# Chunked attention, then a routed expert layer, on one core: another order at the beginning and in the expert loop, w2 loaded later, the first routing spread

## The chip, the cores and the metric

The kernel runs on one core of a Trainium2 chip. The metric is the device time of one execution in microseconds (us), the median of three runs; lower is better. A profile is one further execution, recorded by the hardware profiler.

## The reference

q, k and v have 8 batches, 8 heads, 576 positions and 64 columns, all float32. Attention is local: each chunk of 64 positions attends to itself alone. The heads joined give x (8 x 576 tokens of 512 columns). Each token then goes through one of eight experts:

```python
scores = scale * q_c @ k_c^T ; scores -= max ; attn = exp(scores) / (sum + 1e-9)
x = (attn @ v_c), heads joined: [8, 576, 512]
logits = x @ w_gate                        # [8, 576, 8]
local_gate = sigmoid(x @ w_local)          # [8, 576]
for b, s in order:
    fresh_e = argmax(logits[b, s])
    e = fresh_e if s == 0 or local_gate[b, s] < 0.5 else prev_e
    p = softmax(logits[b, s])
    out[b, s] = p[e] * (relu(x[b, s] @ w1[e]) @ w2[e])   # 512 -> 1024 -> 512
```

Which expert a token gets may hang on the tokens before it, so the routing is a scan.

## The kernel before

**Attention.** The 4608 tokens are 18 tiles of 256 (`NS`). A tile is loaded (`load_qk`, `load_v`, issued by SyncE, SP), q and k are copied so that two heads lie side by side (`a_pair`), transposed by TensorE (PE) and copied out of PSUM (`a_tq`), multiplied to scores, which VectorE (DVE) reduces and shifts and ScalarE (ACT) exponentiates (`a_sa`); the probabilities are transposed (`a_tp`), multiplied with v and normalised (`a_va`), the result is transposed (`a_tx`) and multiplied with the router's columns (`a_ra`), which also stores the tile's rows, logits included, in the DRAM table `x_d`. Tiles 4 and 13 collect the last 64 positions of four batches: their loads and stores come in four small pieces.

**Orders by hand.** Within `manual_schedule` the engines named there execute in the order of the program text. The text is given by strings in `PAR`: `play` takes names of queues and counts, and runs the next atoms of each. `PAR["start"]` is the beginning (tiles 0 to 2), `PAR["steady"]` one step of the loop over i = 1 to 15 (scores of tile i + 1, transposes of tile i + 2, values of tile i - 1, router of tile i - 2), `PAR["drain"]` what follows. PE, DVE and ACT are in that order in all parts, GpSimd (POOL) from the loop on; SP's order is the scheduler's until the expert loop. Letters such as `"AVPA"` in `PAR` say which engine copies (A ACT, V DVE, P POOL).

**First routing.** The first half of the tokens (`TA` = 18 groups of 128) is routed while attention still runs (`route`, with the atoms s1a to s11, then ranks, then one-hot rows). A step of the loop has four places for such work, h0 to h3; `PAR["hooks"]` lists for each piece the step and place as 4 i + h. Then three early tiles of expert 0 are gathered from `x_d` (`early_gather`), whose expert work is done within the drain.

**Weights.** Expert 0's w1 (`raw1`) is loaded after steps 6, 8, 10 and 12 and its w2 (`raw2`, four loads of 512 KB) after steps 13 and 14. Products of float32 precision are made of three passes: a weight is held as a high part (`w1h`, `w2h`, a copy by ACT) and a low part (`w1l`, `w2l`, a difference by DVE or POOL), and so are the activations. `w2_split` in the drain (queue w) makes the parts of expert 0's w2 and loads the next expert's w2 into `raw2`.

**Expert loop.** The tokens are sorted by expert into tiles of 128 rows, in halves of 64; a tile whose halves belong to two experts is mixed. Tile t's step (`step`) does the first product and relu of tile t, the gather of tile t + 2, the high and low parts of the next tile's x (`next_x`), the second product, scaling by the probability and scatter of tile t - 1 (`down`), and h's parts of tile t. Registers read from `regs` say whether the expert changes (row 0), which expert comes (row 1), whether a tile is there at all (row 2, from tile 36, `TMIN`, on) and whether it is mixed (row 3); what hangs on them stands in `tc.If`, on the engines that it uses. `either` chooses between the mixed and the plain products, `rejoin` builds the operands of a mixed tile, `refill` renews the weights' high and low parts where the expert changes and loads the next ones. With these inputs there are 38 tiles, 3 of them mixed.

Of the kernel before, what the change touches and what calls it, by code (L numbers as in the profile page):

```python
# [40 lines left out]
    "start": (  # L41
        "p0*4 t0a*4 t0a t0b*4 t0b t0c*4 t0c t0d*4 t0d p1*4 q3 t1a*4 t1a t1b*4 t1b s0*8 s0*2 t1c*4 t1c "
        "q4 t1d*4 t1d p2*4 s0*4 s1*8 t2a*4 t2a t2b*4 t2b s1*4 o0*4 o0*4 o0 s1*2 t2c*4 o0 t2c t2d*4 t2d q5 p3*4 "
    ),
# [17 lines left out]
    "steady": "lq s*8 s h0 tx*8 s va*4 va tq*8 ra*2 h1 tq*8 va*4 lv va ra*2 h2 tp*8 s pr*4 h3 ",  # L62
    "hooks": [43, 43, 44, 45, 46, 47, 48, 48, 50, 50, 52, 52, 54, 54, 55, 58, 61, 61, 62],
}
# [3 lines left out]
def tile_attention_then_moe(ctx: ExitStack, tc, q, k, v, wg, wl, w1, w2, out):  # L68
# [430 lines left out]
    def run(fns):  # L499
        for fn in fns:  # L500
            fn()

    for t in vbuf:
        nc.gpsimd.memset(t[:, :, :, D:DV], 1.0)
# [7 lines left out]
    nc.sync.dma_start(wg9[:, :, 8:9], wl.rearrange("(c p) e -> p c e", p=P))  # L512
    with tc.manual_schedule(engines=MAN):
        def load(store, fn, i):
            def go():
                store[i] = fn(i)
            return lambda: [go]

        tqs = {}

        def tq(i, g):
            if i not in tqs:
                tqs[i] = a_tq(i, ENG(PAR[f"t{i}"]))
# [3 lines left out]
        st |= dict(  # L527
            s0=lambda: a_sa(0, True), q3=load(qk, load_qk, 3),
            s1=lambda: a_sa(1, True), o0=lambda: a_tp(0, True), q4=load(qk, load_qk, 4), q5=load(qk, load_qk, 5))
# [5 lines left out]
    def iota(shape, pattern, base=0, cm=0, dt=F32, name=None, dst=None):  # L535
        t = cpool.tile(shape, dt, name=name) if dst is None else dst
        nc.gpsimd.iota(t, pattern, base=base, channel_multiplier=cm, allow_small_or_imprecise_dtypes=True)
        return t

    pcol = iota([P, 1], [[0, 1]], cm=1, name="pcol")  # L540
    pcol1 = iota([P, 1], [[0, 1]], base=1, cm=1, name="pcol1")
    iota_r = iota([P, P], [[1, P]], dst=pa2.tile([P, P], BF16, name="iota_r", tag="xT", bufs=1))
    iota_m = iota([P, P], [[0, 2], [1, HT]], dt=BF16, name="iota_m")
    iota_h = iota([P, 2, NTILE], [[1, 2], [2, NTILE]], dt=BF16, name="iota_h")
    iota_hp = cpool.tile([P, NTILE], BF16, name="iota_hp")
    for r in range(2):
        nc.gpsimd.iota(iota_hp[HT * r:HT * r + HT], [[2, NTILE]], base=r, channel_multiplier=0,
                       allow_small_or_imprecise_dtypes=True)
    iota_t = cpool.tile([P, NT], BF16, name="iota_t")
    for ph in range(2):  # L550
        iota(None, [[9, 4], [4, 2], [2, 2]], base=36 * ph, dst=iota_t[:, TA * ph:TA * ph + TA - 2])
        for cp in range(2):
            iota(None, [[9, 2]], base=36 * ph + 18 * cp + 8 - cp,
                 dst=iota_t[64 * cp:64 * cp + 64, TA * ph + TA - 2:TA * ph + TA])
    iota_e = iota([P, E], [[1, E]], name="iota_e")
    idxm8 = iota([P, E], [[1, E]], base=-E, name="idxm8")
    padidx = iota([P, NTILE], [[P, NTILE]], base=2 * N, cm=1, name="padidx")
    upper = pa1.tile([P, P], BF16, name="upper")
    nc.vector.tensor_scalar(upper, iota_r, pcol, None, ALU.is_gt)
    ones = pa1.tile([P, P], BF16, name="ones")  # L560
    nc.gpsimd.memset(ones, 1.0)
    zrow = pa1.tile([P, E * NT], F32, name="zrow")
    nc.gpsimd.memset(zrow, 0.0)
    notfirst = pa1.tile([P, NT], F32, name="notfirst")
    nc.gpsimd.memset(notfirst, 1.0)
    for b in range(B):
        t = TA * (b // 4) + 4 * (b % 4)
        nc.gpsimd.memset(notfirst[0:1, t:t + 1], 0.0)


# [144 lines left out]
    def either(mix, plain, both):  # L715
        if mix is None:
            plain()
            return
        with tc.If(mix != 0) as cmp:
            both()  # L720
        with cmp.Else():
            plain()

# [75 lines left out]

    hot0 = cpool.tile([P, E], F32, name="hot0")  # L800
    nc.gpsimd.memset(hot0, 0.0)
    nc.gpsimd.memset(hot0[:, 0:1], 1.0)

    sg, sg_rank, sg_onehots = route(0, TA, lambda t: nc.gpsimd if t % 2 else nc.vector)
# [7 lines left out]

    hq = sg + [lambda: run(sg_rank()), after_a, lambda: run(sg_onehots())] + sl[:2] + [early_gather] + sl[2:]
    hooks = {}
# [4 lines left out]
    for i in range(1, NS - 2):  # L819
# [8 lines left out]
        if i in (6, 8, 10, 12):  # L828
            load_w1(0, i // 2 - 3)
        if i in (13, 14):  # L830
            for c in range(2 * i - 26, 2 * i - 24):
                load_w2(0, c)
        if 8 <= i < 16:
# [8 lines left out]


    n = NS - 1
    sa = a_sa(n, True)
# [71 lines left out]
    def rejoin(mix, parts, names, last):  # L917
# [7 lines left out]
        pair = pool.tile([P, len(parts), 4, P], F32R, name="pair" + names[0], **tag)  # L925
        with tc.If(mix != 0):  # L926
            for g, part in enumerate(parts):
                for n, a in enumerate(part):
                    V.tensor_copy(pair[:, g, :, HT * n:HT * n + HT], a[:, :, 0:HT])
            for full, (hi, lo) in zip(fulls, parts):  # L930
                V.tensor_tensor(full, hi[:, :, HT:P].bitcast(F32), lo[:, :, HT:P].bitcast(F32), ALU.add)
# [6 lines left out]

    def refill_lo(which, t):
        hi, lo, raw = ((w1h, w1l, raw1), (w2h, w2l, raw2))[which]  # L940
        en = reg(1, t + 1, E - 1, [ET.SP])
        for c in range(4):
            V.tensor_tensor(lo[c], raw[c], hi[c].bitcast(F32), ALU.subtract)  # L943
# [7 lines left out]
    def refill(which, t, between=None):  # L951
# [5 lines left out]
        with tc.If(reg(0, t, 1, [ET.Activation]) != 0):  # L957
            refill_hi(which)
        between()
        with tc.If(reg(0, t, 1, [ET.DVE, ET.SP]) != 0):  # L960
            refill_lo(which, t)

# [13 lines left out]
    def step(t, ok, mix):  # L976
# [21 lines left out]

        def down(cs):
# [91 lines left out]
```

## Time and profile before

| | |
|---|---|
| runs | 679.46, 679.68, 681.99 us (median 679.68) |
| profiled execution | 681.47 us, its span 679.2 us |
| PE busy | 642.6 us, 95% of the span |
| DVE, ACT, POOL busy | 368.2, 268.7, 140.3 us |
| HBM read, written | 76.48 MB, 19.56 MB |

Times in the profile are from the start of the span. Attention fills it to about 160 us, the drain with the second routing to about 205 us, the expert loop the rest. An engine's time counts as busy while an instruction runs on it; the words behind an arrow in a row say what ended the idle time before it. [...]

### The profile page before, as it was taken

Reading aid. Unit: us, or ns where it says so; the run is one execution under the profiler, and the core shown is the slowest. Engines: PE = TensorE matmul, PEld = TensorE weight load, DVE = VectorE, ACT = ScalarE, POOL = GpSimd, SP = SyncE. Lnnn points to the kernel's source line nnn. Section 1 sums busy time; section 2 is a strip of 40 time slices with the busy share of each in tenths; the row PEclk is TensorE's granted clock in tenths of the full one; section 3 lists DMA queues with packets and bytes.
Section 4 is the critical chain, followed back from the end, with each engine's and each line's share of the span. In section 5 each row is a group of like instructions: output and inputs, shape, how many; then the busy total and the mean of one; then the engine's idle time right before and its main releaser. Section 6 shows DMA issues by size and latency. Waiting matters only on the chain. (4 is left out here: it accounts for less than half of the span.)

```text
span 679.2 us, 16236 instructions
## 1 busy us (share of the span) xinstructions
PE 642.6 (95%) x5552; PEld 513.1 (76%) x5552; DVE 368.2 (54%) x939; ACT 268.7 (40%) x432; POOL 140.3 (21%) x208
## 2 busy tenths in 40 slices
PE   4799899979998999999999999999998999999994
PEld 4687687767786888778888886788886888778883
DVE  1577478876784666665323455662475532466231
ACT  2576587755312144532212443422364121343220
POOL 4322244560051111121111121121111111111101
PEclk9899899998999999999999999999999999999998
DMA  9999999995622144234121244451166411145100
GB/s 243 254 240 283 250 266 284 267 284 169 202 93 82 34 156 153 76 138 165 35 65 33 68 153 152 157 168 49 36 225 233 158 33 64 34 157 170 51 20 34
DMA packets 102496, 97.31 MB, mean 143 GB/s; under 512 B 42256, under 2 KB 79120, under 8 KB 102352
## 3 DMA queue, kind: packets, MB, share of 16 engines
q1 hardware_dynamic: 96192, 75.69, 38.1%
q0 software_dynamic: 6160, 19.85, 8.7%
q8 instruction: 72, 1.18, 0.7%
q14 instruction: 72, 0.59, 0.3%
HBM read 76.48 MB, written 19.56 MB: 141 GB/s over the span
## 5 line engine op out<-in xcount | busy, mean ns | idle before, releaser
L694 PE MATMUL y<-w2h,hp 128*128 128x512 f32 x560 | 187.3, 405 | 2.4 <-ACTq L953 2.0
L673 PE MATMUL h<-w1h,xp 128*128 128x512 f32 x560 | 164.0, 402 | 0.0
L694 PEld LDWEIGHTS y<-w2h,hp 128*128 128x128 f32 x560 | 106.6, 190 | 27.3 <-issue 3.3
L673 PEld LDWEIGHTS h<-w1h,xp 128*128 128x128 f32 x560 | 102.5, 189 | 21.8 <-ACTq L953 0.2
L760 POOL DMA_INDIRECT out<-ysb,sidx x38 | 37.8, 995 | 387.0 <-DVE ysb L1007 331.2
L694 PE MATMUL y<-w2l,hp 128*128 128x512 f32 x280 | 112.0, 400 | 2.1 <-DVE w2l L943 2.1
L742 ACT ACTIVATE hsb<-h 128x1024 f32<-128x1024 f32 x35 | 35.9, 1026 | 160.9 <-PE h L673 140.6
L673 PE MATMUL h<-w1l,xp 128*128 128x512 f32 x280 | 88.1, 396 | 1.6 <-DVEq L953 1.6
L641 ACT CAST hp<-tr 128x512 fp32r<-128x512 f32 x76 | 41.2, 589 | 111.0 <-PE tr L639 102.9
L642 DVE TENSOR_TENSOR xp<-tr,xp 128x512 fp32r<-128x512 f32 x39 | 27.0, 691 | 89.5 <-ACT xp L641 85.8
L694 PEld LDWEIGHTS y<-w2l,hp 128*128 128x128 f32 x280 | 53.5, 191 | 14.1 <-DVE w2l L943 2.7
L673 PEld LDWEIGHTS h<-w1l,xp 128*128 128x128 f32 x280 | 52.5, 188 | 14.8 <-DVEq L953 2.0
L642 DVE TENSOR_TENSOR hp<-tr,hp 128x512 fp32r<-128x512 f32 x76 | 49.3, 685 | 18.4 <-ACT hp L641 12.7
L1007 DVE TENSOR_SCALAR ysb<-y,ppr 128x512 f32<-128x512 f32 x32 | 24.0, 750 | 61.7 <-PE y L694 52.0
L639 PE MATMUL tr<-ident,hsb 128*128 128x128 f32 x304 | 40.2, 273 | 0.3 <-ACT hsb L742 0.3
L639 PEld LDWEIGHTS tr<-ident,hsb 128*128 128x128 f32 x304 | 35.3, 140 | 6.7 <-ACT w2h L937 1.2
L645 POOL DMA_INDIRECT xg<-x_d,gidx x36 | 35.6, 990 | 20.7 <-issue 9.5
L212 DVE TENSOR_REDUCE mx<-sc 128x8 f32<-128x512 f32 x36 | 23.2, 685 | 23.4 <-PE sc L201 23.4
L943 DVE TENSOR_TENSOR w2l<-raw,w2h 128x1024 fp32r<-128x1024 f32 x28 | 32.4, 1220 | 5.6 <-DVEq L926 4.9
L943 DVE TENSOR_TENSOR w1l<-raw,w1h 128x1024 fp32r<-128x1024 f32 x28 | 32.4, 1221 | 5.3 <-ACT w1h L937 5.3
L937 ACT CAST w2h<-raw 128x1024 fp32r<-128x1024 f32 x28 | 28.5, 1046 | 14.4 <-PE y L700 5.8
L250 PE MATMUL o<-v,pT 64*64 64x65 f32 x1152 | 28.1, 234 | 4.0 <-DVE xs L264 2.9
(195 smaller groups left out, 833.0 us busy)
## 6 DMA issues: line engine op xcount, KB each, us to landing
raw<-in_moe_w SPq DMA_DIRECT2D x72, 512.0 KB, 3.7
x_d<-xs SPq DMA_DIRECT2D x16, 521.0 KB, 5.3
v<-in_v SPq DMA_DIRECT2D x32, 256.0 KB, 4.9
qt<-in_q SPq DMA_DIRECT2D x15, 512.0 KB, 5.6
kt<-in_k SPq DMA_DIRECT2D x15, 512.0 KB, 7.4
x_d<-xs SPq DMA_DIRECT2D x8, 130.2 KB, 4.9
qt<-in_q SPq DMA_DIRECT2D x8, 128.0 KB, 4.8
kt<-in_k SPq DMA_DIRECT2D x8, 128.0 KB
```

Of the source, the lines that this page charges most:

```text
L250: nc.tensor.matmul(o[64 * cp:64 * cp + 64, cc, DV * h:DV * h + D + 1], pT[64 * cc:64 * cc + 64, 4 * j + h, 64 * cp:64 * cp + 64], vt[64 * ...
L639: nc.tensor.transpose(ps[:, n], src_of(n), ident)
L641: return [tr, lambda: nc.scalar.copy(hi, box["ps"]), lambda: V.tensor_tensor(lo, box["ps"], hi.bitcast(F32), ALU.subtract)]
L642: lambda: V.tensor_tensor(lo, box["ps"], hi.bitcast(F32), ALU.subtract)]
L645: nc.gpsimd.indirect_dma_start(out=dst, out_offset=None, in_=src, in_offset=bass.IndirectOffsetOnAxis(ap=gidx[t].bitcast(U32), axis=0))
L673: nc.tensor.matmul(hs[:, j], xs[a][:, c], W1[w][c][:, 512 * j:512 * j + 512], start=(c == 0 and n == 0), stop=(c == 3 and n == 2))
L694: nc.tensor.matmul(y, hx[f // 4][a][:, f % 4], W2[w][c][:, f % 2, :], start=(f == 0 and n == 0), stop=(f == 7 and n == 2))
L742: nc.scalar.activation(hsb, hs.rearrange("p j f -> p (j f)"), AF.Relu)
L760: nc.gpsimd.indirect_dma_start(out=out, out_offset=bass.IndirectOffsetOnAxis(ap=sidx[t].bitcast(U32), axis=0), in_=ysb, in_offset=None, bo ...
L937: nc.scalar.copy(hi[c], raw[c])
L943: V.tensor_tensor(lo[c], raw[c], hi[c].bitcast(F32), ALU.subtract)
L1007: V.tensor_scalar(ysb, y, pr, None, ALU.mult)
```

## The change

It makes these edits:

- Beginning: the constants on POOL (`constants`) stand behind the copies of tile 1 in an order that now includes POOL; one comparison goes from DVE to POOL; ACT begins with an Exp on one column of the identity; the first tile's transposed probabilities are copied ahead of the second tile's exponentials.
- First routing: other hooks; the ranks in two parts, the one-hot rows in three.
- Expert 0's w2 is loaded behind the loop instead of after steps 13 and 14.
- Expert loop: in `either` the plain case stands first; `rejoin`'s condition is for DVE alone; the refill of w2's low parts is done half before and half behind h's parts; the rest of the probabilities is worked out behind the refill of w1.
- Exit: the case in which tile t is not there stands first, begins with a DRAIN of POOL, and shares the last scaling between DVE and ACT.

```diff
-        "q4 t1d*4 t1d p2*4 s0*4 s1*8 t2a*4 t2a t2b*4 t2b s1*4 o0*4 o0*4 o0 s1*2 t2c*4 o0 t2c t2d*4 t2d q5 p3*4 "
+        "q4 t1d*4 t1d p2*4 s0*4 s1*8 t2a*4 t2a t2b*4 t2b s1*2 o0*4 o0 o0*4 o0 s1*2 t2c*4 t2c t2d*4 t2d s1*2 q5 p3*4 "
...
-        "p0*4 t0a*4 t0a t0b*4 t0b t0c*4 t0c t0d*4 t0d p1*4 q3 t1a*4 t1a t1b*4 t1b s0*8 s0*2 t1c*4 t1c "
+        "p0*4 t0a*4 t0a t0b*4 t0b t0c*4 t0c t0d*4 t0d p1*4 io q3 t1a*4 t1a t1b*4 t1b s0*8 s0*2 t1c*4 t1c "
...
-    "hooks": [43, 43, 44, 45, 46, 47, 48, 48, 50, 50, 52, 52, 54, 54, 55, 58, 61, 61, 62],
+    "hooks": [43, 43, 45, 46, 47, 48, 49, 49, 51, 51, 52, 53, 54, 55, 55, 56, 57, 58, 59, 61, 61, 62],
...
-    with tc.manual_schedule(engines=MAN):
+    with tc.manual_schedule(engines=MAN | {ET.Pool}):
+        warm = cpool.tile([P, 1], F32, name="warm")
+        nc.scalar.activation(warm, ident[:, 0:1], AF.Exp)
...
+            io=lambda: [constants], s0=lambda: a_sa(0, True), q3=load(qk, load_qk, 3),
...
-    nc.vector.tensor_scalar(upper, iota_r, pcol, None, ALU.is_gt)
+        nc.gpsimd.tensor_scalar(upper, iota_r, pcol, None, ALU.is_gt)
...
-        with tc.If(mix != 0) as cmp:
-            both()
-        with cmp.Else():
-            plain()
+        with tc.If(mix == 0) as cmp:
+            plain()
+        with cmp.Else():
+            both()
...
+    late = {}
+
+    def part_of(key, fn, n, m):
+        def go():
+            if key not in late:
+                late[key] = fn()
+            fns = late[key]
+            run(fns[len(fns) * n // m:len(fns) * (n + 1) // m])
+        return go
+
-    hq = sg + [lambda: run(sg_rank()), after_a, lambda: run(sg_onehots())] + sl[:2] + [early_gather] + sl[2:]
+    hq = sg + [part_of("rank", sg_rank, n, 2) for n in range(2)] + [after_a]
+    hq += [part_of("oh", sg_onehots, n, 3) for n in range(3)] + sl[:2] + [early_gather] + sl[2:]
...
-        if i in (13, 14):
-            for c in range(2 * i - 26, 2 * i - 24):
-                load_w2(0, c)
...
+    for c in range(4):
+        load_w2(0, c)
     n = NS - 1
...
-        with tc.If(mix != 0):
+        with tc.If(nc.snap(mix, engines=[ET.DVE]) != 0):
...
-    def refill_lo(which, t):
+    def refill_lo(which, t, cs=range(4)):
...
         with tc.If(reg(0, t, 1, [ET.Activation]) != 0):
             refill_hi(which)
+        with tc.If(reg(0, t, 1, [ET.DVE, ET.SP]) != 0):
+            refill_lo(which, t, (0, 1))
         between()
         with tc.If(reg(0, t, 1, [ET.DVE, ET.SP]) != 0):
-            refill_lo(which, t)
+            refill_lo(which, t, (2, 3))
...
-                if cs[-1] == 3:
+                if cs[-1] == 3 and shared:
+                    V.tensor_scalar(ysb[:, 0:256], y[:, 0:256], pr, None, ALU.mult)
+                    nc.scalar.mul(ysb[:, 256:C], y[:, 256:C], pr)
+                elif cs[-1] == 3:
                     V.tensor_scalar(ysb, y, pr, None, ALU.mult)
...
-            with tc.If(ok[t] != 0) as cmp:
+            with tc.If(ok[t] == 0) as cmp:
+                with when(ok[t - 1]):
+                    nc.gpsimd.drain()
+                    down((0, 1, 2, 3), True)
+            with cmp.Else():
                 down((0, 1))
                 next_h(0)
                 down((2, 3))
-            with cmp.Else():
-                with when(ok[t - 1]):
-                    down((0, 1, 2, 3))
...
-        run(pr)
         full[0, t] = rejoin(mix[t], [xps[t]], "x", t == TMIN + 3)
         refill(0, t - 1)
+        run(pr)
```

## Rows read from the trace of the kernel before

**Rows 1.** Busy time by stretch: stretch, length, engines' busy us, PE's clock, DMA share, GB/s.
```profile
100.00:120.00 20.00, 19.01 (x420) 14.74 (x415) 17.18 (x53) 14.99 (x27) 10.00 (x14) 1.00 1.06 286
120.00:140.00 20.00, 17.17 (x405) 13.77 (x400) 16.89 (x56) 12.59 (x23) 12.07 (x20) 1.00 1.03 277
148.00:151.10 3.10, 1.18 (x20) 0.65 (x15) 1.18 (x8) 1.44 (x2) 2.73 (x3) 0.95 1.21 295
340.00:360.00 20.00, 20.00 (x96) 16.31 (x95) 5.82 (x19) 4.29 (x8) 2.96 (x4) 1.00 0.18 55
```

**Rows 2.** The same view, three stretches of lower granted clock.
```profile
75.70:79.10 3.40, 3.40 (x45) 2.95 (x44) 3.06 (x7) 1.17 (x2) 0.00 (x0) 0.50 0.93 214
150.80:157.60 6.80, 6.54 (x83) 5.19 (x87) 3.55 (x7) 2.55 (x5) 0.74 (x1) 0.50 0.48 169
526.30:529.60 3.30, 3.30 (x8) 2.62 (x9) 3.30 (x4) 0.00 (x0) 0.00 (x0) 0.50 0.47 160
```

**Rows 3.** Timeline, 5.9 to 13.2 us: start, duration, engine, line, operation, tiles [idle before].
```profile
6.08 1.28 ACT L162 ACT_TABLE_LOAD   x1 [6.08 <-DMA qt<-in_q]
8.14 1.94 PE L172 MATMUL tr<-ident,qr 128*128 128x128 f32 x8 [8.14 <-ACT qr L162]
8.31 0.22 POOL L537 IOTA pcol<- 128x1 f32 x2
12.01 1.15 POOL L164 COPY qr<-qt 128x512 f32<-128x512 f32 x2
```

**Rows 4.** Timeline, 14 to 36 us, PE.
```profile
25.31 0.63 PE L172 MATMUL tr<-ident,kr 128*128 128x128 f32 x4 [2.30 <-ACT pT L162]
27.25 1.50 PE L201 MATMUL sc<-kT,qT 64*64 64x64 f32 x64 [1.31 <-ACT kT L162]
```

**Rows 5.** Timeline, 126 to 152 us, the one-hot rows and PE behind them.
```profile
132.39 1.82 DVE L452 TENSOR_SCALAR rh<-iota_m,rq 128x128 bf16<-128x128 bf16 x9
137.69 0.70 PE L250 MATMUL o<-v,pT 64*64 64x65 f32 x32 [1.82 <-DVE xs L264]
```

**Rows 6.** The same timeline, SP's issues.
```profile
141.83 2.08 SPq L95 DMA_DIRECT2D raw<-in_moe_w  x2
147.78 3.45 SPq L316 DMA_DIRECT2D x_d<-xs  x4
```

**Rows 7.** Timeline, 151 to 186 us: v's last load and the first copy of w2.
```profile
157.96 1.46 SPq L144 DMA_DIRECT2D v<-in_v  x2
160.14 1.07 ACT L839 CAST w2h<-raw 128x1024 fp32r<-128x1024 f32 x1
```

**Rows 8.** The page, DMA issues: count, KB each, median us from issue to landing.
```profile
raw<-in_moe_w SPq DMA_DIRECT2D x72, 512.0 KB, 3.7
v<-in_v SPq DMA_DIRECT2D x32, 256.0 KB, 4.9
```

**Rows 9.** Timeline, 216 to 222 us, PE.
```profile
220.18 0.73 PE L673 MATMUL h<-w1l,xp 128*128 128x512 f32 x2 [1.61 <-DVEq L953]
```

**Rows 10.** Timeline, 516 to 527 us, the change of expert.
```profile
525.02 2.36 DVE L943 TENSOR_TENSOR w2l<-raw,w2h 128x1024 fp32r<-128x1024 f32 x2 [0.69 <-DVEq L926]
526.29 0.79 PE L694 MATMUL y<-w2l,hp 128*128 128x512 f32 x1 [2.14 <-DVE w2l L943]
```

**Rows 11.** Timeline, 657 to 680 us, the last tile's second product.
```profile
664.83 0.47 PE L694 MATMUL y<-w2h,hp 128*128 128x512 f32 x1 [1.96 <-ACTq L953]
```

**Rows 12.** Branches on PE, by line: ns shortest/median/longest, first and last start.
```profile
L719 PEldq COMPARE_BRANCH  x78: 68/210/370, 205.9 to 664.4; - x78
...
L1024 PEldq COMPARE_BRANCH  x2: 507/1366/2226, 658.6 to 663.7; - x2
```

**Rows 13.** Timeline, 62 to 79 us, PE.
```profile
74.89 0.57 PE L201 MATMUL sc<-kT,qT 64*64 64x64 f32 x22 [2.67 <-issue]
```

**Rows 14.** Timeline, 126 to 152 us: a load of v, and the next product with v.
```profile
124.80 2.45 SPq L144 DMA_DIRECT2D v<-in_v  x2
...
132.10 0.69 PE L250 MATMUL o<-v,pT 64*64 64x65 f32 x31
```

More of the change, by code (lines that the diff above doesn't have):

```diff
@@ L501, in run, with iota, constants @@
             fn()
+    def iota(shape, pattern, base=0, cm=0, dt=F32, name=None, dst=None):
+        t = cpool.tile(shape, dt, name=name) if dst is None else dst
+        nc.gpsimd.iota(t, pattern, base=base, channel_multiplier=cm, allow_small_or_imprecise_dtypes=True)
+        return t
+    const = {}
+    def constants():
+        pcol = iota([P, 1], [[0, 1]], cm=1, name="pcol")
+        pcol1 = iota([P, 1], [[0, 1]], base=1, cm=1, name="pcol1")
+        iota_r = iota([P, P], [[1, P]], dst=pa2.tile([P, P], BF16, name="iota_r", tag="xT", bufs=1))
+        iota_m = iota([P, P], [[0, 2], [1, HT]], dt=BF16, name="iota_m")
+        iota_h = iota([P, 2, NTILE], [[1, 2], [2, NTILE]], dt=BF16, name="iota_h")
+        iota_hp = cpool.tile([P, NTILE], BF16, name="iota_hp")
+        for r in range(2):
+            nc.gpsimd.iota(iota_hp[HT * r:HT * r + HT], [[2, NTILE]], base=r, channel_multiplier=0,
+                           allow_small_or_imprecise_dtypes=True)
+        iota_t = cpool.tile([P, NT], BF16, name="iota_t")
+        for ph in range(2):
+            iota(None, [[9, 4], [4, 2], [2, 2]], base=36 * ph, dst=iota_t[:, TA * ph:TA * ph + TA - 2])
+            for cp in range(2):
+                iota(None, [[9, 2]], base=36 * ph + 18 * cp + 8 - cp,
+                     dst=iota_t[64 * cp:64 * cp + 64, TA * ph + TA - 2:TA * ph + TA])
+        iota_e = iota([P, E], [[1, E]], name="iota_e")
+        idxm8 = iota([P, E], [[1, E]], base=-E, name="idxm8")
+        padidx = iota([P, NTILE], [[P, NTILE]], base=2 * N, cm=1, name="padidx")
+        upper = pa1.tile([P, P], BF16, name="upper")
+        nc.gpsimd.tensor_scalar(upper, iota_r, pcol, None, ALU.is_gt)
+        ones = pa1.tile([P, P], BF16, name="ones")
+        nc.gpsimd.memset(ones, 1.0)
+        zrow = pa1.tile([P, E * NT], F32, name="zrow")
+        nc.gpsimd.memset(zrow, 0.0)
+        notfirst = pa1.tile([P, NT], F32, name="notfirst")
+        nc.gpsimd.memset(notfirst, 1.0)
+        for b in range(B):
+            t = TA * (b // 4) + 4 * (b % 4)
+            nc.gpsimd.memset(notfirst[0:1, t:t + 1], 0.0)
+        hot0 = cpool.tile([P, E], F32, name="hot0")
+        nc.gpsimd.memset(hot0, 0.0)
+        nc.gpsimd.memset(hot0[:, 0:1], 1.0)
+        const.update(pcol=pcol, pcol1=pcol1, iota_m=iota_m, iota_h=iota_h, iota_hp=iota_hp, iota_t=iota_t, iota_e=iota_e, idxm8=idxm8, padidx=padidx, upper=upper, ones=ones, zrow=zrow, notfirst=notfirst, hot0=hot0)
@@ L527, in tile_attention_then_moe @@
         st |= dict(
-            s0=lambda: a_sa(0, True), q3=load(qk, load_qk, 3),
+            io=lambda: [constants], s0=lambda: a_sa(0, True), q3=load(qk, load_qk, 3),
             s1=lambda: a_sa(1, True), o0=lambda: a_tp(0, True), q4=load(qk, load_qk, 4), q5=load(qk, load_qk, 5))
@@ L533, in tile_attention_then_moe @@
         play(PAR["start"], st)
[L535 to L558, printed above, removed]
-    nc.vector.tensor_scalar(upper, iota_r, pcol, None, ALU.is_gt)
[L560 to L568, printed above, removed]
+    pcol, pcol1, iota_m, iota_h, iota_hp, iota_t, iota_e, idxm8, padidx, upper, ones, zrow, notfirst, hot0 = (
+        const[n] for n in "pcol pcol1 iota_m iota_h iota_hp iota_t iota_e idxm8 padidx upper ones zrow notfirst hot0".split())
     gidx, sidx = {}, {}
@@ L798, in early_m2 @@
         return [lambda c=c: mm2(hps[t], y, c) for c in range(4)] + [lambda: emit_y(t, y, prc[t])]
-    hot0 = cpool.tile([P, E], F32, name="hot0")
-    nc.gpsimd.memset(hot0, 0.0)
-    nc.gpsimd.memset(hot0[:, 0:1], 1.0)
     sg, sg_rank, sg_onehots = route(0, TA, lambda t: nc.gpsimd if t % 2 else nc.vector)
@@ L937, in refill_hi @@
             nc.scalar.copy(hi[c], raw[c])
-    def refill_lo(which, t):
+    def refill_lo(which, t, cs=range(4)):
         hi, lo, raw = ((w1h, w1l, raw1), (w2h, w2l, raw2))[which]
         en = reg(1, t + 1, E - 1, [ET.SP])
-        for c in range(4):
+        for c in cs:
             V.tensor_tensor(lo[c], raw[c], hi[c].bitcast(F32), ALU.subtract)
@@ L997, in step, with down @@
         y, ym = (new_y(), new_m()) if t > EARLY else (None, None)
-        def down(cs):
+        def down(cs, shared=False):
             pr = prc[t - 1]
```

## The prediction

> **What bounds the kernel now.** Read first the busy time by stretch. In the expert loop TensorE (PE) has 20.00 us of work in 20.00 us [rows 1]; nothing taken off another engine there can show, except where PE itself waits. So the second view is PE's idle time, read from the timeline, with the engine that ended each wait: the beginning, a few steps of the attention, one place in the loop and the exit have such waits. [...] A stretch at half clock gives back half its length if it goes: 1.7 us for 3.4 us, 3.4 us for 6.8 us. The change is priced wait by wait. The sum is made against the profiled execution, 681.47 us (span 679.2 us and 2.3 us around it). The runs shown are 679.46, 679.68 and 681.99 us, so the profiled one belongs to the longer ones; it stands 1.8 us above their median, about one short half-clock stretch.
>
> **The change part by part.**
>
> *Beginning.* Three waits of PE are touched. (i) The table load of 1.28 us stands between q's landing (6.08) and ACT's first copy, and PE's first transpose (8.14) follows that copy [rows 3]. An Exp on the identity matrix pays the load while ACT waits for data: the first transpose comes 1.28 us earlier. (ii) POOL builds constants from 8.31 to about 12.0, and its copies for tile 1 start only then (12.01) [rows 3]; PE's next transposes wait for them. With the copies ahead of the constants PE goes from tile 0's two groups of transposes (1.94 us each at half clock) nearly straight on. Together: tile 1's transposes start at 8.14 - 1.28 + 2 x 1.94 = 10.7 us instead of behind the first of POOL's two copies, 12.01 + 1.15 / 2 = 12.6, and what follows, tile 1's scores too, is 1.9 us earlier. (iii) PE then waits 2.30 us for the copy of tile 0's transposed probabilities and 1.31 us for the copies of k [rows 4]; ACT had them behind tile 1's exponential, which waits for four DVE operations. In the new order ACT copies both halves first. The DVE operations stay, so one exponential and two k copies still close the chain: I get tile 2's scores at about 24.0 instead of 27.25, that is 3.2 us for the whole part. The constants (3.7 us, with the comparison that DVE did) now lie before POOL's copies of tile 2, which end near 17.2 and are needed near 18.5: hidden by 1.3 us. Bounds: 0, if loads and not PE set this stretch, and -4.9 with a half-clock stretch of 3.4 us gone too. I take **-3.2**.
>
> *First routing.* In 100:140 PE is idle for 0.99 + 2.83 us [rows 1]. The worst place is the lump of rank, offsets and one-hots at the end of one step: nine one-hots hold DVE for 1.82 us, so the work on the next scores starts late, and PE waits 1.82 us at 137.69 for the normalised values that stand behind it [rows 5]. Now the ranks come in two parts and the one-hots in three (three on DVE, some 0.6 us, each); the transposes get a hook more of room after their inputs. DVE's work is the same, and over these steps it has little room, so not all of it goes: between +0.5 and -3.8, I take **-2.5**.
>
> *Expert 0's w2.* Two of the four loads leave from 141.83 and two some 8 us before; x_d's four small stores leave from 147.78 [rows 6], and from 148.0 to 151.1 PE dribbles through the scores, busy for 1.18 of 3.10 us [rows 1], in short waits that no semaphore explains. That is 1.9 us, and 6.8 us at half clock follow [rows 2]. Transfers fill the DMA engines here (277 GB/s in 120:140, share 1.03 [rows 1]); I hold these waits for code that arrives late behind data. Moved behind the loop, the 2 MB leave that stretch: up to 1.9 + 3.4 = 5.3 us gained. The price: SP issues the loads behind x_d's stores. ACT first reads w2 at 160.14 [rows 7], 12.4 us after the stores began; without those 5.3 us it is 7.1 us after. The stores take 3.45 us to issue, the first load lands 3.7 us (the median of weight loads [rows 8]) or more later, so at 7.2 to 9.4; the next follow at 0.52 MB / 277 GB/s = 1.9 us each, and ACT wants the second 2.6 us after the first. ACT would wait up to 2.3 us, and PE behind it. Bounds: -5.3, and +4 if SP issues the loads only behind v's last one (157.96 [rows 7]): the first then lands at 161.7, 1.5 us behind ACT's present read, each later one more so, and what was gained is paid back ahead of it. I take -5.3 + 2.3 = **-3.0**.
>
> *Expert loop.* Probabilities behind refill: at 220.18 PE waits 1.61 us for DVE to pass the condition of the first refill, behind five small operations of the probabilities [rows 9]. These go behind it: 0.8 us, which is their length. Bounds 0 and -1.6; **-0.8**. Half of w2's low parts ahead of the h parts: at 526.29 PE waits 2.14 us for the first low part, which DVE starts at 525.02 [rows 10], though its inputs are there from 519; 3.4 us at half clock follow [rows 2]. In the new order the first two run in DVE's idle time before 523, and the third ends at 526.2, when PE, started at 523.9, wants it at 526.7. Bounds 0 and -3.8, I take **-3.8** (2.14 + 1.65). Elsewhere in the loop PE has no wait, so these edits are free there; what covers the h parts, now 2.4 us later on DVE, is PE's 5.6 us of the next tile's first product. Tests of the mixed flag go from PE and ACT: PE's queue hides them, nothing. DVE gets one more condition per step, some 0.7 us of its sequencer, hidden likewise.
>
> *Exit.* After the last tile's h, PE spends 1.96 us in branches before y [rows 11]. One is removed and one no longer jumps (0.51 us against 0.21 for a median one [rows 12]): -0.6. The last scaling split over DVE and ACT: -0.3 of 0.75 us. DVE's extra condition lies on the way to the last jump: +0.7 of which half is covered by the scatter. POOL's drain, at a place where POOL waits 8 us for y anyway, costs nothing. **-0.5**, between +0.7 and -2.3 (with a half-clock stretch gone).
>
> Sum: -3.2 - 2.5 - 3.0 - 0.8 - 3.8 - 0.5 = -13.8, so 667.7 us; I say 667.5 us.
>
> **The rivals.**
>
> *The stall near 148 stays.* What for: a like wait, 2.67 us, stands at 74.89 [rows 13] with 3.4 us at half clock behind it [rows 2], also at four small stores of x_d, with no w2 load near. Against: in the second place the loads are the one thing more in the queues. Then the -5.3 us is lost, nothing is saved by the move, ACT's wait shrinks to about nothing: 667.7 + 3.0 = 670.7, say 671 us. [...]
>
> *Loads of v become the bound.* v's pair for the tile of the step at 130 us is issued until 124.80 + 2.45 = 127.25 [rows 14], lands 4.9 us later at the median [rows 8], at 132.15, and PE's product with v starts at 132.10 [rows 14]. For: there is no slack to see. Against: no wait on v shows, and SP issues these loads after PE's releases, so they come earlier with PE. Of the 5.7 us of the first two parts up to 4.5 would be lost: 672 us.
>
> *More goes than counted.* The wait at 74.89 is a matter of how code and stores meet; a beginning that is shifted may undo it: another 2.67 + 1.7 = 4.4 us, 663 us.
>
> *w2 too late.* SP's order is not written out here; if the loads fall behind v's last one, the upper bound of that part holds: 667.7 + 3.0 + 4 = 675, up to 678 us with a half-clock stretch kept.
>
> *Branches come into the open.* The unmixed part now comes first, and every engine jumps over the mixed one after it instead of before. PE executes 78 such branches at 0.21 us [rows 12]; were each to delay the next product, 16 us would be lost: 667.7 + 16.4 = 684 us, slower. It decides where PE's queue holds less work than a branch takes. Against it: in the tail a branch of PE took 2.2 us [rows 12] and no idle time of PE stands there. [...]
>
> **How the numbers follow.** Forecast 0.43 (its own range 664 to 671), stall stays 0.20, v the bound 0.14, more goes 0.07, w2 too late 0.09, branches 0.07. Range 660 to 677.5 us: above it lie the branches and the far end of "w2 too late", below it the far end of "more goes". A change under 0.5% (3.4 us) can't be told from none: faster (under 676.3 us) in the first four cases, 0.84; the same 0.09, "w2 too late"; slower 0.07, the branches.
>
> **What would show it.** Right: PE's first transpose near 6.9 and tile 2's scores near 24; no PE wait of over 1 us between 100 and 145; no half clock after x_d's second set of small stores; ACT's first w2 copy with a wait on its load; no PE wait on w2l or half clock near 520 us; PE's last wait before y near 1.4 us. Wrong: a wait on v in steps 11 to 14, waits of PE's own queue after unmixed products, PE waiting behind w2h in the drain, or new half-clock stretches in the loop.

## The result: 672.13 us against 678.56 us, and the profile after

The changed kernel took 672.13 us at the median of 10 executions (670.08 to 674.30), the kernel before 678.56 us at the median of 10 (674.36 to 681.99, those shown ahead among them). The ratio is 0.990, 95% interval 0.9875 to 0.9925: 6.4 us faster, where 667.5 us had been forecast, 11 us under this median and 12 under that of the three executions shown. The time lies inside the range; about half of the forecast gain is missing. The profiled execution took 674.20 us, with a span of 672.4 us.

The two profiles at the same points of the work, in us from the start:

| point | before | after | lead | gained since the point above |
|---|---|---|---|---|
| tile 2's scores begin | 27.25 | 22.82 | 4.43 | 4.43 |
| tile 12's scores begin | 104.93 | 102.00 | 2.93 | -1.50 |
| tile 17's scores begin | 147.24 | 146.09 | 1.15 | -1.78 |
| PE goes on after the first refill | 220.18 | 217.05 | 3.13 | 1.98 |
| PE goes on before the last y | 664.83 | 657.57 | 7.26 | 4.13 |
| end of the span | 679.2 | 672.4 | 6.8 | -0.46 |

Rows of the timeline after that answer to [rows 3, 4, 9, 11]; the columns are start, duration, engine, line, operation, tiles, and in brackets the idle time before it and what ended it:

```profile
6.53 1.94 PE L172 MATMUL tr<-ident,qr 128*128 128x128 f32 x8 [6.53 <-ACT qr L162]
22.82 1.16 PE L201 MATMUL sc<-kT,qT 64*64 64x64 f32 x64 [1.60 <-ACT kT L162]
217.05 0.74 PE L684 MATMUL h<-w1l,xp 128*128 128x512 f32 x2 [0.69 <-DVEq L970]
520.67 2.36 DVE L960 TENSOR_TENSOR w2l<-raw,w2h 128x1024 fp32r<-128x1024 f32 x2 [0.67 <-DVEq L943]
657.57 0.47 PE L705 MATMUL y<-w2h,hp 128*128 128x512 f32 x1 [1.16 <-ACTq L992]
```

The first transpose is 1.6 us earlier, the first refill costs PE 0.69 us instead of 1.61, and at the change of expert DVE works on w2's last low parts at 520.67 without PE waiting: the wait of 2.14 us at 526.29 [rows 10] and the half clock behind it are gone (granted clock 1.00 from 523 to 530 us).

What is new in the attention are more waits of PE that no semaphore explains ("issue"). Up to 145 us the profile before has two of over 0.25 us, 0.89 at 66.39 and 2.67 at 74.89 [rows 13]; now there are six, and a wait of 0.84 us for DVE at 112.34. The four longest:

```profile
47.16 0.47 PE L201 MATMUL sc<-kT,qT 64*64 64x64 f32 x17 [1.86 <-issue]
72.44 0.57 PE L201 MATMUL sc<-kT,qT 64*64 64x64 f32 x22 [1.58 <-issue]
107.85 0.59 PE L292 MATMUL lg<-xT,wg 128*32 128x256 f32 x2 [1.46 <-issue]
132.23 0.21 PE L250 MATMUL o<-v,pT 64*64 64x65 f32 x1 [1.77 <-issue]
```

The same kernel by stretch (stretch, length, busy us of PE, PEld, DVE, ACT, POOL with their counts, granted clock as a share of full speed, DMA share, GB/s); the first two answer to [rows 2], the third to the stall in [rows 1]:

```profile
47.70:51.00 3.30, 3.30 (x43) 2.85 (x43) 2.82 (x6) 1.17 (x2) 0.00 (x0) 0.50 0.94 217
133.00:136.40 3.40, 3.40 (x21) 2.17 (x19) 3.31 (x11) 1.58 (x3) 3.40 (x7) 0.50 0.10 32
146.80:149.60 2.80, 0.94 (x7) 0.60 (x8) 1.16 (x8) 2.21 (x4) 1.95 (x3) 1.00 1.16 300
```

Two new half-clock stretches (granted clock 0.50) follow the waits at 47.16 and 132.23, and the stall near 148 stands as before: PE is busy for 0.94 us of 2.80.

### The profile page after: what moved, and what is told of

Read it like the earlier page. It is cut to its first block, busy times and chain, and to the rows that moved or that the text cites. A ratio compares the mean times of both kernels' runs of the same rounds, so it can differ in the third digit from the quotient of the medians.

```text
span 672.4 us, 16746 instructions
## 1 busy us (share of the span) xinstructions
PE 638.5 (95%) x5552; PEld 509.7 (76%) x5552; DVE 371.6 (55%) x938; ACT 271.6 (40%) x434; POOL 147.1 (22%) x209
## 5 line engine op out<-in xcount | busy, mean ns | idle before, releaser
L705 PE MATMUL y<-w2h,hp 128*128 128x512 f32 x560 | 185.3, 401 | 1.6 <-ACTq L992 1.2
L771 POOL DMA_INDIRECT out<-ysb,sidx x38 | 43.7, 1151 | 374.0 <-DVEq L976 269.9
L705 PEld LDWEIGHTS y<-w2h,hp 128*128 128x128 f32 x560 | 105.0, 188 | 26.2 <-issue 2.5
L705 PE MATMUL y<-w2l,hp 128*128 128x512 f32 x280 | 110.5, 395 | 0.0
L212 DVE TENSOR_REDUCE mx<-sc 128x8 f32<-128x512 f32 x36 | 23.2, 685 | 20.4 <-PE sc L201 20.4
```

The costliest lines, as they stand in the source:

```text
L705: nc.tensor.matmul(y, hx[f // 4][a][:, f % 4], W2[w][c][:, f % 2, :], start=(f == 0 and n == 0), stop=(f == 7 and n == 2))
L771: nc.gpsimd.indirect_dma_start(out=out, out_offset=bass.IndirectOffsetOnAxis(ap=sidx[t].bitcast(U32), axis=0), in_=ysb, in_offset=None, bo ...
```

## The experiments

"Late code" in the expectations is the guess that PE waits for its own instructions where these arrive late; the last section has what the traces show of it. The kernel before took 679.3, 677.9, 673.1 and 676.7 us at the median on the four chips used, so only ratios on one chip are compared. One per cent is 6.8 us.

**One part at a time.** On one chip the kernel before with each of four parts alone. The beginning (order of the tokens, constants as one step, table load on the identity matrix):

```diff
+        warm = cpool.tile([P, 1], F32, name="warm")
+        nc.scalar.activation(warm, ident[:, 0:1], AF.Exp)
-  "p0*4 ... p1*4 q3 t1a*4 ... t2b*4 t2b s1*4 o0*4 o0*4 o0 s1*2 ..."
+  "p0*4 ... p1*4 io q3 t1a*4 ... t2b*4 t2b s1*2 o0*4 o0 o0*4 o0 s1*2 ..."
```

> The kernel before with the new beginning alone (order, constants, table load). Theory 'late code': while the DMA engines are full (share 1.0 from 5 to 130 us), PE runs ahead of its own instruction blocks, and the 4.4 us won at tile 2's scores (27.25 to 22.82 in the changed kernel) are given back in new idle stretches of PE that end on nothing a semaphore shows, before 150 us: total change 0 to -2 us. Rival 'sum': a beginning that is earlier shifts all that follows, total change -3.2 to -4.4 us.

Measured: 0.9962 (0.9934 to 0.999), that is -2.6 us (-0.7 to -4.5). This interval covers the ranges of both expectations, so the time can't choose; the traces can. Tile 2's scores began at 23.29, 2.0 us ahead of the mean of the three other traces of this chip, and tile 12's 1.9 us ahead of them (101.55 against 103.45). The lead is not eaten. Over all chips tile 12's scores begin at 103.8 us on average in four traces with the old beginning, at 101.1 in eight with the new one. What shrank is the start: 27.25 in the profile before was late. Four other traces with the old beginning have 25.0 to 25.5; this is the row of the next experiment:

```profile
25.26 1.45 PE L201 MATMUL sc<-kT,qT 64*64 64x64 f32 x64 [1.30 <-ACT kT L162]
```

Over all traces it is 23.2 with the new beginning (nine) against 25.7 with the old (five), 2.5 us, as the time says. "Sum" stands with a smaller lead than it had taken from the first two profiles; "late code" falls for this part.

w2's loads behind the attention loop:

```diff
-        if i in (13, 14):
-            for c in range(2 * i - 26, 2 * i - 24):
-                load_w2(0, c)
+    for c in range(4):          # behind the loop
+        load_w2(0, c)
```

> The kernel before with expert 0's w2 loads behind the attention loop alone. Theory 'late code': the short waits near 148 us are not caused by w2's loads (the changed kernel has them too, 1.88 us against 1.91), so they stay; fewer bytes ahead of 148 may shorten a code wait by up to 1 us; total change within 1 us of none. Rival of the prediction: the waits and the half clock behind them go, and ACT waits up to 2.3 us for w2: -3 us.

Measured: 1.0002 (0.9973 to 1.0032). The edit did less than it says. SP's order is the scheduler's, and only two of the four loads (line 95 is `load_w2`) left behind x_d's small stores; the other two still left ahead of them, at 139.81. The short waits stand at the same place:

```profile
139.81 1.60 SPq L95 DMA_DIRECT2D raw<-in_moe_w  x2
148.59 1.90 SPq L95 DMA_DIRECT2D raw<-in_moe_w  x2
146.88 0.31 PE L201 MATMUL sc<-kT,qT 64*64 64x64 f32 x3 [0.37 <-issue]
147.66 0.35 PE L201 MATMUL sc<-kT,qT 64*64 64x64 f32 x3 [0.48 <-issue]
148.43 0.35 PE L201 MATMUL sc<-kT,qT 64*64 64x64 f32 x4 [0.41 <-issue]
149.16 0.59 PE L201 MATMUL sc<-kT,qT 64*64 64x64 f32 x10 [0.38 <-issue]
```

This trace alone does not clear w2. The kernel before with fewer bytes (the next group of runs) does: there SP sent all four loads some 65 us earlier, and the waits stand all the same:

```profile
67.32 1.60 SPq L95 DMA_DIRECT2D raw<-in_moe_w  x2
77.03 2.06 SPq L95 DMA_DIRECT2D raw<-in_moe_w  x2
149.60 0.34 PE L203 MATMUL sc<-kT,qT 64*64 64x64 f32 x3 [0.40 <-issue]
```

The changed kernel with fewer bytes has them too (0.41 us at 147.56), with its w2 loads sent by 76.2. So w2 does not make them, and its move is worth nothing that the time shows (-1.8 to +2.2 us).

The first routing's hooks, with ranks and one-hots in parts:

```diff
-    "hooks": [43, 43, 44, 45, 46, 47, 48, 48, 50, 50, 52, 52, 54, 54, 55, 58, 61, 61, 62],
+    "hooks": [43, 43, 45, 46, 47, 48, 49, 49, 51, 51, 52, 53, 54, 55, 55, 56, 57, 58, 59, 61, 61, 62],
-    hq = sg + [lambda: run(sg_rank()), after_a, lambda: run(sg_onehots())] + ...
+    hq = sg + [part_of("rank", sg_rank, n, 2) for n in range(2)] + [after_a]
+    hq += [part_of("oh", sg_onehots, n, 3) for n in range(3)] + ...
```

> The kernel before with the new hooks and the split lumps of the first routing alone. Theory 'late code': DVE's waits at 128.12 and 137.69 (0.76 and 1.82 us) go, but PE then reaches the ends of its code blocks sooner and waits there; total change 0 to -1.5 us. Rival 'sum': the 2.5 us of DVE waits go and nothing comes for them: -2.5 us.

Measured: 0.9994 (0.9963 to 1.0026). Nothing gained that the time shows (-2.5 to +1.8 us), and a wait of 1.84 us for normalised values stands in this trace too, now at 144.21. The experiments further down say more.

The edits of the expert loop (unmixed part first, refill in halves, probabilities behind the refill):

```diff
-        with tc.If(mix != 0) as cmp: both() ... Else: plain()
+        with tc.If(mix == 0) as cmp: plain() ... Else: both()
+        with tc.If(reg(0, t, 1, [ET.DVE, ET.SP]) != 0):
+            refill_lo(which, t, (0, 1))
         between()
         with tc.If(reg(0, t, 1, [ET.DVE, ET.SP]) != 0):
-            refill_lo(which, t)
+            refill_lo(which, t, (2, 3))
-        run(pr)          # now behind refill(0, t - 1)
```

> The kernel before with the edits of the expert loop alone (unmixed part first, refill in two halves, probabilities behind the refill). Both theories: DMA share is 0.45 here and no code wait shows, so the gains stand: 0.9 us at 220 and 2.14 + 1.65 us at 526, total -4.0 to -4.7 us. Rival 'branches': the unmixed part first makes PE jump later, total not below -1 us.

Measured: 0.9926 (0.9893 to 0.996), -5.0 us (-2.7 to -7.3). From the first refill's wait to the last y's, eight traces with these edits take 440.0 to 440.8 us, four without 442.4 to 445.3 (mean 444.0). With the 0.9 us at the refill that is 4.4 us by the means. PE's waits at w2's refill near 509 and 524 us, 2.1 us in the profile before, are 1.3, 1.7 and 2.7 us in the other three of these four, and none over 0.15 us stands there in the eight with them. No trace shows PE waiting behind a branch in the loop.

**Fewer bytes.** Both kernels with v's loads left out for tiles 4 to 15 (values, and so the routing, differ):

```diff
     def load_v(i):
         vt = vbuf[i % NV]
+        if 4 <= i < 16:
+            return vt
```

> The changed kernel with the loads of v left out for tiles 4 to 15 (they use v of tiles 2 and 3; the values and so the routing differ): 6.3 MB of some 39 MB less up to 150 us, PE's own work in the attention unchanged. Theory 'late code': with the DMA engines no longer full, PE's 16 KB code blocks come in time; the waits at block ends (7.5 us in all between 39 and 133) and the two half-clock stretches behind them go, tile 17's scores start near 136 instead of 146.09. Rival 'the fetch itself is slow': the waits at block ends stay, tile 17's scores at 144 to 146. The number of mixed tiles may differ, so the attention's end is compared, not the total.

> The kernel before with the same loads of v left out. Theory 'late code': its waits at block ends (3.8 us, with 1.7 us of half clock) go, DVE's waits at 128 and 137 (2.6 us) stay or grow: tile 17's scores near 142 instead of 147.24, and the changed kernel's lead there grows from 1.2 us to about 5 us, which is what the beginning and the hooks were priced at. Rival: the lead stays 1 to 2 us, since something else eats the gain.

Measured, at tile 17's scores: 146.13 us with the change and 148.24 without. (The totals, 724.51 and 739.50 us, belong to another routing.) Neither came to the expected 136 and 142: the attention did not get shorter. The waits at code blocks did become fewer where the DMA share fell. The changed kernel with fewer loads, by stretch:

```profile
75.00:100.00 25.00, 24.30 (x551) 20.03 (x550) 16.47 (x42) 17.96 (x31) 9.61 (x14) 0.97 0.79 228
100.00:125.00 25.00, 23.78 (x527) 18.71 (x529) 19.90 (x64) 18.19 (x32) 10.88 (x16) 1.00 0.51 159
125.00:146.00 21.00, 18.15 (x416) 14.80 (x408) 20.20 (x65) 13.65 (x25) 13.16 (x20) 1.00 0.15 54
```

Ahead of 75 us, where later loads had moved up and the DMA share was still 1.05 (25 to 75 us), it has three waits without a semaphore (1.31, 1.69 and 2.68 us); behind it one of 0.70 and one of 0.23, none from 103 to 146. The kernel before with fewer loads has none from 76 to 146, but with all its loads it has none there either, so that pair says nothing; the count over all traces is in the last section. What holds this end is DVE, busy for 20.20 of 21.00 us:

```profile
136.39 0.70 PE L252 MATMUL o<-v,pT 64*64 64x65 f32 x32 [2.73 <-DVE xs L266]
```

So two limits lie behind one another here, and taking away the bytes left the other.

**The exit.** The changed kernel with the exit of before, and with its last scaling alone put back (the diff shows the second):

```diff
-                    down((0, 1, 2, 3), True)     # DVE scales columns 0 to 255, ACT the rest
+                    down((0, 1, 2, 3))           # DVE scales all
```

> The changed kernel with the exit of the kernel before (last scaling on DVE alone, no drain of POOL, order of the tail's branches as before). From the end of PE's last wait to the end of the program the profiles show 14.4 us before (1.7 us of it half clock) and 14.8 us after (none): the exit as changed is dearer by some 2 us, so this kernel is 1.5 to 2 us faster than the changed one, ratio to before 0.987 to 0.988. Rival, as the prediction priced it: the changed exit saves 0.5 us, this kernel is 0.5 us slower than the changed one, 0.991.

> The changed kernel with only the last scaling back on DVE alone. In the changed kernel ACT's half starts when DVE's has ended (664.13 behind 663.61 + 0.48), so the split costs 0.3 us on the way to the last scatter. Theory 'the split alone': the 2 us at the exit go with it. Rival 'the branches': only 0.3 us goes, and the far jump of 4.22 us and DVE's late last instructions stay.

Measured: 0.9893 (0.9857 to 0.9929) and 0.9859 (0.9822 to 0.9897). Against 0.990 for the whole change the times can't settle 1.5 us, the difference expected. The traces can. From PE's last wait to the end, in the changed kernel, in its second trace, with the scaling put back, and with the loop's edits alone (exit of before):

```profile
657.57:672.40 14.83, 5.83 (x24) 4.39 (x24) 0.73 (x2) 0.47 (x1) 1.48 (x2) 0.77 0.12 40
```

```profile
657.08:671.40 14.32, 5.83 (x24) 4.39 (x24) 0.82 (x2) 0.47 (x1) 1.57 (x2) 0.79 0.12 41
```

```profile
658.33:671.20 12.87, 5.82 (x24) 4.39 (x24) 1.01 (x2) 0.00 (x0) 1.49 (x2) 0.90 0.14 46
```

```profile
659.19:672.00 12.81, 5.78 (x24) 4.41 (x24) 0.95 (x2) 0.00 (x0) 1.21 (x2) 0.87 0.13 46
```

PE's 24 products take the same 5.8 us in all four. Both traces with the split scaling take 14.3 to 14.8 us, the eight without it and without half clock under the products 12.8 to 13.0 (v's loads left out aside). Against the mean of these eight, 12.86, the split costs 1.4 to 2.0 us, and its undoing takes all of that away ("the split alone"; the tail's branches cost nothing that shows). One part is in the rows of the changed kernel:

```profile
663.61 0.48 DVE L1026 TENSOR_SCALAR ysb<-y,ppr 128x256 f32<-128x256 f32 x1 [5.80 <-PEq L992]
664.13 0.47 ACT L1027 ACTIVATE ysb<-y,ppr 128x256 f32<-128x256 f32 x1 [7.06 <-DVE ysb L1026]
664.88 0.97 POOL L771 DMA_INDIRECT out<-ysb,sidx  x1 [6.81 <-DVEq L976]
```

ACT starts when DVE has ended, and its row names DVE's half as what released it: the two halves read one tile and write one tile, and they run one after the other, 0.99 us with the gap instead of 0.75. The rest is at DVE's very last instruction: it comes 2.1 us after DVE's step ahead of it (669.98 to 672.09), in the second trace 1.7 us after (669.32 to 671.04); with the scaling put back 0.1 us. The other engines wait 1.8 and 1.4 us for it. That DVE waits for code there is an inference from the likeness to PE's waits (a code packet of 8 KB landed 1.9 and 1.5 us before that instruction); no row names it.

**Once more, and other hooks.** On a third chip the changed kernel unchanged; with the scaling put back and the old hooks and lumps; and with the scaling put back, the old early hooks and the new small parts:

```diff
 best1: "hooks" and hq as before;  down((0, 1, 2, 3))
 best2: "hooks": [43, 43, 44, 45, 46, 47, 48, 48, 50, 50, 52, 52, 53, 54, 55, 56, 57, 58, 59, 61, 61, 62]
```

> The changed kernel once more, unchanged: a second trace of the same program. Theory 'full DMA': how long each wait at a block end is differs from execution to execution, and some may turn into waits for v's loads, but all stand where PE's instruction count is a multiple of 256 from the first, and PE's waits between 27.5 and 146 us sum to 8 to 11 us again (9.4 in the first trace). Rival 'fixed places': the same waits at 47.16, 72.44, 107.85 and 132.23 us with the same lengths to 0.2 us. At the exit: the 2.1 us that DVE's last drain was late (669.98 to 672.09) comes again if it belongs to the split scaling's code, and is absent if it was chance. Ratio 0.990.

> The changed kernel with the last scaling on DVE alone and with the first routing's hooks and lumps of the kernel before. Theory 'the new hooks cost': from the scores of the step that begins at 102 to tile 17's scores the four traces with new hooks take 44.1 to 45.2 us, those with the old ones 42.3 to 43.7: this kernel is 1 to 2 us faster than the one with only the scaling undone, ratio 0.983 to 0.985. Rival 'full DMA decides': what the hooks give or take is given back in code or v waits, ratio 0.986 as before.

> As the changed kernel with the last scaling on DVE alone, but the routing's steps up to the column counts at the old, earlier hooks, and ranks and one-hots spread over the hooks behind them (rank in two parts at 53 and 54, one-hots at 56, 57, 58). Theory: the ranks' 3.2 us on DVE (127.4 to 130.6 in the trace with the scaling undone) then fall ahead of the next scores, and PE's wait of 2.3 us for the normalised values shrinks below 1 us, the half clock behind it goes: 2 to 3 us faster than with the new hooks, ratio 0.981 to 0.983. Rival: DVE's work over these steps is the same and it has no idle time from 123 to 139 us, so the wait only moves; ratio 0.985 to 0.987.

Measured: 0.9902 (0.9866 to 0.9938), 0.989 (0.9856 to 0.9924) and 0.9919 (0.989 to 0.9948): the three can't be told apart, so neither set of hooks is shown to be faster, and what was expected of the second and third kernel (0.983 to 0.985 and 0.981 to 0.983) did not come. In the traces, from tile 12's scores to tile 17's (v's loads left out aside), five traces with the new hooks take 43.1 to 45.2 us (mean 44.3), six with the old ones 42.3 to 43.7 (mean 42.9), and the mixed ones 44.1. The expected 1 to 2 us is seen there, but not in the time.

Why the new hooks don't help stands in the trace of the changed kernel with the scaling put back:

```profile
128.75 0.18 DVE L446 TENSOR_SCALAR ri<-ri 128x18 int32<-128x18 int32 x1
128.81 1.27 POOL L99 TENSOR_TENSOR w1l<-raw,w1h 128x512 fp32r<-128x512 f32 x1 [2.71 <-ACT w1h L98]
128.84 1.27 DVE L447 TENSOR_SCALAR ri<-ri 128x18 int32<-128x18 int32 x1
130.15 0.18 DVE L448 CAST rq<-ri 128x36 f32<-128x36 int32 x1
130.63 1.27 DVE L212 TENSOR_REDUCE mx<-sc 128x8 f32<-128x512 f32 x2
134.68 0.70 PE L250 MATMUL o<-v,pT 64*64 64x65 f32 x32 [2.32 <-DVE xs L264]
```

A step of the ranks that takes 0.17 us before takes 1.27 us, as long as POOL's split of w1 beside it, and ends 0.03 us after that: it is held, as such steps are called here. The next row maximum starts some 1.1 us later, and PE waits 2.32 us for what follows. The same coincidence is in both traces of the changed kernel (1.14 us at 130.14, 1.26 at 129.50), in that with the old exit (1.28 at 128.94) and in that with fewer loads (1.29 at 130.55). The kernel with the hooks alone escaped it there by 0.2 us and was held later, ahead of the wait at 144.21: its last three one-hots, beside POOL's copies, took 1.77 us instead of 0.57, and the two comparisons behind them, beside the next split, 1.48 instead of 0.33:

```profile
137.03 1.77 DVE L452 TENSOR_SCALAR rh<-iota_m,rq 128x128 bf16<-128x128 bf16 x3
138.72 1.48 DVE L583 TENSOR_TENSOR qeq<-qsA,iota_h 128x54 bf16<-128x54 f32 x2
138.72 1.27 POOL L99 TENSOR_TENSOR w1l<-raw,w1h 128x512 fp32r<-128x512 f32 x1
```

The mixed kernel was held at that place too (1.28 us at 135.62), with a wait of 1.85 us at 140.48.

In the seven traces with the old hooks no step of the ranks is held: there POOL's nine one-hots are queued ahead of that split of w1 and push it behind the ranks (137.54 in the profile before). But DVE is held there as well, in a copy of the logits, behind the values that PE waits for, and no PE wait for DVE follows up to tile 17's scores; this is the profile before, where that copy takes 0.18 us by itself:

```profile
139.79 1.27 DVE L310 COPY xs<-L 128x18 f32<-128x18 f32 x1
```

From tile 12's scores to tile 17's, steps that took over 0.25 us more than usual add 2.3 to 2.5 us to DVE in the seven traces with the old hooks, 2.1 to 3.9 in the six with the new ones and 4.4 in the mixed one. So the place of the holds changed, and not always their sum. Not every step is held: row maxima over the scores took their usual 0.7 us beside an earlier split (114.00 in the changed kernel). The held steps beside the splits take some 1.1 us more each; why DVE is held there and not elsewhere the traces don't show. It was seen in traces, not tried: no kernel here moved that split alone.

The second trace of the changed kernel settles the places of the code waits too: none at 107.85 and 132.23, one of 2.41 us at 71.76, one of 0.70 at 90.75; in sum PE's waits of over 0.25 us between 27.5 and 146 us are 9.25 us against 9.44, of which 5.1 and 7.5 us have no semaphore. "Fixed places" falls.

**Two parts alone.** The kernel before with the beginning and the loop's edits, on a fourth chip (the diffs above):

> The kernel before with two of the five parts alone, those that moved the time by themselves: the new beginning (0.9962) and the edits of the expert loop (0.9926); w2's place, the routing's hooks and the exit as before. Theory 'the parts add up and the other three give nothing': ratio 0.986 to 0.990, so no slower than the whole change (0.990 and 0.9902), and a span from PE's last wait to the end of 12.8 to 13 us. Rival 'the parts need each other' (w2 out of the full stretch, the spread hooks): ratio above 0.992. The short waits near 148 us should be there or not by the chip, not by the kernel.

Measured: 0.9895 (0.9844 to 0.9945), so not shown to be slower than the whole change, with three of its five parts left out; exit 12.8 us. No kernel here is shown to beat the changed one: the lowest ratio, 0.9859 with the scaling put back, overlaps with it.

**The stall near 148.** It is in all eight traces of two chips, for kernels of before and after, with w2's loads there or not, and in both first profiles; in none of the four traces of two other chips, the unchanged changed kernel among them:

```profile
148.25 0.77 PE L172 MATMUL tr<-ident,pr 128*128 128x128 f32 x5 [0.59 <-ACT pr L220]
```

This is PE's first wait after tile 17's scores there (146.50 to 147.66 without a gap). What makes it on some chips stays open; it isn't at a code block's end.

## Why the prediction was half right

- **Beginning, -3.2.** Right in mechanism, -2.6 measured. The first eight transposes, which the prediction has at half clock, take 1.94 us in both profiles at a granted clock of 1.00 (8.10 to 10.10 us before, 6.50 to 8.50 after), while eight take 1.09 at 20.34 in the profile before; what makes them slow is not shown. Between the two profiles the part is -4.4, but in the profile before tile 2's scores were 1.8 to 2.2 us behind other executions, with the first transpose no later than in those (8.1 to 8.3). The half-clock stretch that the prediction let stay is no fixed thing: it is at 27.9 to 31.3 in the profile before, at 16.9 to 20.3 in that after, and three of the nine traces with the new beginning have none there.
- **First routing, -2.5: the step that failed in its mechanism.** The prediction held that smaller lumps let DVE reach the next scores sooner, and wrote "DVE's work is the same". Its work is, but not where it is held: the new order lets short steps of DVE meet long ones of POOL ahead of values that PE waits for, at 1.1 us in the ranks, or as much or more behind them. Measured -0.4 us (-2.5 to +1.8). That these holds eat the gain is read from the traces, not tried. The later hooks also gave a new wait of 0.84 us, at 112.34, for DVE's sc (line 369).
- **w2, -3.0: failed,** in two steps. "Moved behind the loop, the 2 MB leave that stretch" came half true: in the changed kernel two of the loads leave at 139.47, ahead of x_d's small stores (from 146.52), and two behind them, at 149.13. And "I hold these waits for code that arrives late behind data": the waits near 148 are at no end of a code block, and w2 has no part in them. ACT did not wait for w2 at all where 2.3 us were priced; its first copy, at 157.94, follows on the copy ahead of it. The rival "the stall near 148 stays" was the truth. That its 671 us came so near is luck in part: it has some 4 us from the first routing and the exit that did not come, and the median of the kernel before is 2.9 us under the profiled execution from which it starts. The half clock behind it did shrink from 6.8 to 3.4 us between the two profiles, but with this part alone it is 6.8 us again (148.8 to 155.7) and no time was won.
- **Expert loop, -4.6 together.** Right: -0.9 at the first refill, the wait at 526 and its half clock gone, -4.4 by traces and -5.0 by time. The half clock near 526, 1.65 us of the price, was in that one profile; none of the three other traces without the edits has it there. The 4.4 us also hold some 0.5 us of the wait before the last y, which was priced at the exit.
- **Exit, -0.5: wrong sign.** The wait before y did shrink, by 0.8 us where 0.6 was priced: 1.96 us before, 1.43 with the loop's edits alone, 1.16 with the tail's branches too, so 0.3 us belong to the exit's own edits. Behind it the split costs 1.4 to 2.0 us, which makes +1.1 to +1.7 in all. The step that failed is "the last scaling split over DVE and ACT: -0.3": it took for granted that both work at once, and no row showed two engines on one tile.
- **The other rivals.** PE waited for v in six traces (5.9 us in the worst, with the old exit), in the changed kernel's two not at all; "loads of v become the bound" is a thing of single executions. "Branches come into the open" and "w2 too late" did not come. "More goes" did not: 1.58 us at 72.44 stands for the 2.67 us at 74.89 [rows 13].

By the times of the parts: -2.6 + 0.1 - 0.4 - 5.0 = -7.9 us, and +1.1 to +1.7 for the exit by the traces, so -6.8 to -6.2 against -6.4 measured. Each time has an interval of some 2 us to either side, so the fit is closer than the parts can promise.

## What to carry to other kernels

Before an order is changed on one engine, look at what the same tokens queue on its neighbour: a short step that lands beside another engine's long instruction can take that one's time (1.27 us instead of 0.17 here), and it matters where in the order this falls. Before a load is said to have moved, read in the new trace when it left. A split of one tile over two engines is parallel only if the trace shows them side by side (here one ran after the other, 0.99 us instead of 0.75). And price a part against several executions: the one profile before held some 2 us of bad luck at the beginning alone, which looked like a gain of the change.

## What the runs showed of the hardware

PE's code comes in blocks, and PE stops at the end of some of them: up to 160 us 23 code packets of 16 KB land in each of the two profiles, while PE passes 23 ends of 256 instructions. Counts of PE's work between two such waits, in the changed kernel, and in the kernel with the loop's edits alone (the two counts of a row are PE and PEld):

```profile
47.16:72.43 25.27, 23.69 (x505) 19.34 (x504) 15.76 (x39) 16.40 (x27) 7.06 (x12) 0.93 1.03 266
72.44:107.84 35.40, 33.30 (x756) 26.83 (x757) 25.52 (x66) 25.29 (x43) 14.40 (x21) 1.00 1.03 262
107.85:132.22 24.37, 21.67 (x506) 17.59 (x506) 19.78 (x63) 16.69 (x29) 10.63 (x15) 1.00 1.08 281
```

```profile
74.76:115.73 40.97, 39.49 (x882) 32.16 (x883) 30.18 (x84) 29.41 (x50) 15.61 (x24) 0.96 1.04 266
115.74:134.52 18.78, 16.39 (x380) 13.19 (x380) 15.90 (x54) 12.74 (x22) 9.32 (x14) 1.00 1.04 274
```

1009, 1513, 1012, 1765 and 760 counted instructions are 4, 6, 4, 7 and 3 times 252 to 253; with the uncounted ones of PE's sequencer the waits lie 256 apart or a multiple of it, to one instruction: all 45 of over 0.25 us between 27 and 145 us that no semaphore explains, in the fourteen traces of before, after and the runs. The page's row for PE's code:

```profile
q8 instruction: 73, 1.20, 0.7%
```

is 16 KB a packet, and such a packet had landed 1.2 to 1.7 us before each of the 45 ended. They cost 0.3 to 2.7 us each. In the 7 us before each of the 45 the DMA share was 0.85 to 1.15. Most ends of blocks, 226 of 271, have no such wait: the fourteen traces have 271 of them in that time, 249 behind a share of over 0.8, with all 45 waits, and 22 behind a lower share, with none, where 4 would be expected at the same rate. In the expert loop, where the share is 0.33 (200 to 660 us), no such wait is over 0.3 us; PE also goes through its instructions more slowly there, some 10 in a us against 40, so the loop alone does not single out the share. That PE waits for the packet is inferred from this; why it would come late, asked for late or served late, the traces don't show. The wait of 2.67 us that the prediction put down to code and stores [rows 13] is one of them; that stores have a part in it no run shows.
